# Delta rule and two feed-forward layers on one core: low weight parts among the rows of a small inverse, one chunk's steps half a unit later, one transpose a unit sooner

## The chip, the core and the metric

The kernel runs on one core of a Trainium2 chip. The metric is the device time of one execution in microseconds (us), as a median over runs. A profiled execution also gives a trace: start and length of each instruction on TensorE (PE in the rows), VectorE (DVE), ScalarE (ACT), GpSimd (POOL), and of the DMA issues on SyncE (SP).

## The reference, cut to what matters

```python
for t in range(S):                                  # S = 768, per batch (4) and head (8), D = 48
    y[t]  = q[t] @ state
    v_old = state @ k_n[t]                          # k_n: k over its norm
    state = state + beta[t] * outer(k_n[t], v[t] - v_old)
x = y, heads side by side                           # 3072 tokens x 384
h = x @ w_in;   x1 = (h if h > 0 else exp(h) - 1) @ w_out     # d_ff = 2048
h = x1 @ w2_in; out = (h * sigmoid(1.702 * h)) @ w2_out
```

## The kernel before

**Feed-forward.** The 3072 tokens are six passes p of 512. The work is cut into units, one for each layer, pass and block m of 128 of the 2048 inner features; 16 units make a pass, 192 are all. In a unit `up` makes nine 128x512 products into the tile `h` (L785), ScalarE and VectorE turn `h` into `t` and split it into a high part `gh` (L817, ScalarE) and a low part `gl` (L820, VectorE), and two units later (LAG = 2) `down` makes nine products into `acc` (L832). Each number is carried as high and low part, so a product of two numbers is three matmuls: high-high, low-high, high-low. Weights are split too. For block m VectorE puts bits together (`shift` L750, `rest` L753), ScalarE casts the high part (`high`, L760), VectorE subtracts (`low`, L764). The third matmul of `up` is the first to read the low part. At the end of a pass `end_x1` copies the three sums `acc` out: sum 0 and half of sum 1 on VectorE (L893), sum 2 and then the other half of sum 1 on ScalarE (L891). The next pass's `down` writes the same three banks.

**Delta rule.** Tokens are also cut into 12 chunks c of 64, two to a pass. For each pass a triangular inverse is made on VectorE: `take`, `diag`, `norm`, `scale`, then rows (for passes 0 to 2 a "fine" inverse of 14 row steps, L332 and L337 each; for later ones 30 steps, L322 and L327), then `finish` (L344, L345) and a closing transpose `turn` (L351). The fine ones are then joined by `join16`: `turned` (L399), `left` (L410 on TensorE, L414 on ScalarE), `right` (L425). Chunks follow with `kq` (L519), the diagonal steps `t2`, `m1` (L457, L459), `m2` (L472), then `ks` (L587), `w` (L604), `state` (L627, added up in L635), `ya`, `yb` (L664, L680). `kq`, `m2`, `ks`, `w`, `state` and `ya`/`yb` share one wide place `ps_w` in the accumulation memory. `gram` (L218) reads the keys of a chunk from a tile with tag `kg`.

**What sets the order.** Every engine works through its own list in the order in which the code writes it. The pool `ap` has one buffer for a tag unless told otherwise, and the closing transpose of pass 2 writes a tile with tag `kg`, the same buffer from which the grams of chunks 6 and 7 are read. In unit t the code goes: `up(t)`, ScalarE's first half, the list `fill[t]`, `gl` of unit t-1, the list `mid[t]`, VectorE's first step on `t`, `down(t-2)`, the list `end[t]`, the cast to `gh`, the list `tail[t]`. A slot s of a chunk is half a unit: even slots go to `mid` of unit s/2, odd ones to `end`. In pass 2 (chunks 4 and 5) slots count from unit 16. Gram 6 stands in `end` of unit 16, gram 7 in `end` of unit 17, the first half of `join16` of chunk 4 in `mid` of unit 18. The first two inverses are made ahead of the units, except for the rows of the second, which are the list `beside`.

## Time and profile before

| what | us |
|---|---|
| median of 3 runs (lowest, highest) | 964.88 (964.67, 966.6) |
| profiled execution, its own time | 963.57 |
| its span in the trace | 961.8 |
| TensorE busy in the span | 933.4 (97%) |
| VectorE busy | 589.7 (61%) |
| ScalarE busy | 466.1 (48%) |

The span runs from the first to the last instruction; 1.77 us of the profiled execution's time lie around it. In a row of a timeline stand: start in us, length in us, engine, line, operation, tile written <- tiles read, sizes, count, and in brackets how long the engine had been idle before it and what released it. Where a row has a count over one, its length covers them all.

### The profile page before, as it was taken

How to read it: one execution, taken by the hardware profiler on the slowest of the kernel's cores; microseconds unless marked ns; L12 is line 12 of the kernel's file. 1: busy time of each engine (PE TensorE's matmuls, PEld its weight loads, DVE VectorE, ACT ScalarE, POOL GpSimd, SP SyncE). 2: the span in 40 equal slices, each digit the busy share in tenths (PEclk: the TensorE clock that was granted, in tenths of full speed). 3: DMA queues.
4: the chain of work that ended last, by engine and by line, in shares of the span. 5: the costliest groups of instructions: out<-in, count | busy, mean ns of one | idle time of the engine just before them, and what ended most of it. 6: DMA issues, size and time to landing. Idle time of an engine off the chain costs nothing.

```text
span 961.8 us, 25675 instructions
## 1 busy us (share of the span) xinstructions
PE 933.4 (97%) x11529; PEld 766.2 (80%) x11529; DVE 589.7 (61%) x1061; ACT 466.1 (48%) x751; POOL 59.6 (6%) x62
## 2 busy tenths in 40 slices
PE   5888999999999999999999999999999999999998
PEld 4866777788878878887888888888888888888886
DVE  6989997778788877884346766633333333333333
ACT  6777766444654464444447765433333333333332
POOL 3111200100010010000000101001001001010000
PEclk9999999999999999999999999999999999999999
DMA  7475444022211302111019310010020000100000
GB/s 227 156 220 161 116 139 118 4 79 64 94 57 57 90 36 79 63 49 36 1 68 366 158 66 1 1 66 0 1 66 1 34 33 0 66 1 1 34 1 33
DMA packets 22046, 68.33 MB, mean 71 GB/s; under 512 B 3376, under 2 KB 4912, under 8 KB 21936
## 3 DMA queue, kind: packets, MB, share of 16 engines
q1 hardware_dynamic: 18768, 58.30, 18.2%
q10 hardware_dynamic: 3168, 8.39, 3.0%
q8 instruction: 90, 1.47, 0.6%
q14 instruction: 20, 0.16, 0.1%
HBM read 57.25 MB, written 9.44 MB: 69 GB/s over the span
## 4 chain that ended last, share of the span: by engine, by line
PE 86%; DVE 8%; ACT 2%; issue 2%; DMA 1%; DVEq 0%
PE h L785 38%; PE acc L832 27%; PE accn L832 10%; PE ps_w L587 1%; PE ps_w L604 1%; PE ps_w L519 1%; PE ps_w L664 1%; PE ps_w L680 1%; PE ps_w L627 1%; DVE tmp L332 1%; DVE W L337 1%; DVE gl L820 1%; DVE t L808 1%; ACT z L208 1%; DVE x L540 1%
## 5 line engine op out<-in xcount | busy, mean ns | idle before, releaser
L785 PE MATMUL h<-xh,wt 128*128 128x512 f32 (+1 forms) x1158 | 393.1, 394 | 2.2 <-DVE wt L764 1.8
L832 PE MATMUL acc<-gh,wt 128*128 128x512 f32 x864 | 292.5, 393 | 0.0
L785 PEld LDWEIGHTS h<-xh,wt 128*128 128x128 f32 x1158 | 216.8, 188 | 49.8 <-DVE wt L764 2.9
L785 PE MATMUL h<-xl,wt 128*128 128x512 f32 (+1 forms) x579 | 225.5, 389 | 0.6 <-DVE xl L691 0.6
L820 DVE TENSOR_TENSOR gl<-t,gh 128x512 fp32r<-128x512 f32 x192 | 138.4, 721 | 86.0 <-ACT gh L817 86.0
L832 PEld LDWEIGHTS acc<-gh,wt 128*128 128x128 f32 x864 | 162.3, 188 | 34.6
L817 ACT CAST gh<-t 128x512 fp32r<-128x512 f32 x192 | 119.2, 621 | 126.6 <-DVE t L808 67.8
L832 PE MATMUL acc<-gl,wt 128*128 128x512 f32 x432 | 168.7, 390 | 0.0
L814 DVE TENSOR_TENSOR t<-t,h 128x512 f32<-128x512 f32 x96 | 66.0, 688 | 163.9 <-ACT t L811 163.7
L811 ACT ACTIVATE t<-h 128x512 f32<-128x512 f32 x96 | 57.3, 597 | 184.5 <-PE h L785 184.3
L785 PEld LDWEIGHTS h<-xl,wt 128*128 128x128 f32 x579 | 108.8, 188 | 21.7 <-DVE xl L691 0.8
L804 ACT ACTIVATE t<-h 128x512 f32<-128x512 f32 x96 | 57.3, 597 | 87.7 <-PE h L785 87.2
L832 PE MATMUL accn<-gh,wt 128*128 128x512 f32 x288 | 96.5, 389 | 0.0
L808 DVE SCALAR_TENSOR_TENSOR t<-t,h 128x512 f32<-128x512 f32 x96 | 65.6, 684 | 48.3 <-ACT t L805 47.9
L832 PEld LDWEIGHTS acc<-gl,wt 128*128 128x128 f32 x432 | 81.2, 188 | 16.5 <-DVE gl L820 0.4
L832 PEld LDWEIGHTS accn<-gh,wt 128*128 128x128 f32 x288 | 54.1, 188 | 11.2
L805 ACT ACTIVATE t<-t 128x512 f32<-128x512 f32 x96 | 60.7, 632 | 3.1
L832 PE MATMUL accn<-gl,wt 128*128 128x512 f32 x144 | 56.1, 389 | 0.0
L859 POOL TENSOR_TENSOR xl<-x1r,xh 128x512 fp32r<-128x512 f32 x18 | 23.6, 1309 | 405.3 <-ACT xh L858 314.1
L753 DVE SCALAR_TENSOR_TENSOR w<-raw,w 128x768 uint32<-128x768 uint32 x32 | 32.8, 1026 | 0.8
L760 ACT CAST wt<-w 128x768 fp32r<-128x768 f32 x32 | 26.5, 827 | 12.9 <-DVE w L753 12.8
L327 DVE TENSOR_TENSOR W<-W,tmp 128x30 f32<-128x30 f32 (+14 forms) x90 | 29.9, 333 | 3.1
(206 smaller groups left out, 809.9 us busy)
## 6 DMA issues: line engine op xcount, KB each, us to landing
raw<-in_w SPq DMA_DIRECT2D x19, 768.0 KB, 9.6
raw<-in_w ACTq DMA_DIRECT2D x21, 384.0 KB, 3.1
kt<-in_kT SPq DMA_DIRECT2D x12, 512.0 KB, 4.2
x<-in_qT SPq DMA_DIRECT2D x24, 256.0 KB, 4.3
kn<-in_kn SPq DMA_DIRECT2D x12, 384.0 KB, 3.4
x1d<-xo SPq DMA_DIRECT2D x12, 384.0 KB, 2.6
x1r<-x1d SPq DMA_DIRECT2D x6, 768.0 KB, 5.3
vn<-in_vn SPq DMA_DIRECT2D x11, 384.0 KB, 3.6
```

Source lines behind the costliest of these rows:

```text
L327: v.tensor_tensor(out=w, in0=w, in1=t, op=ALU.add)
L753: v.scalar_tensor_tensor(out=bits[m], in0=words(m, 0), scalar=29, in1=bits[m], op0=ALU.logical_shift_right, op1=ALU.bitwise_or)
L760: nc.scalar.copy(wt[:, 0], bits[m].bitcast(F32))
L785: self.nc.tensor.matmul(hps[:, r], wt[:, part, k * P:(k + 1) * P], src[:, k, r], start=(i == 0), stop=(i == 3 * NK - 1))
L804: nc.scalar.activation(out=t, in_=hps, func=AF.Relu, scale=-1.0)
L805: nc.scalar.activation(out=t, in_=t, func=AF.Exp, scale=-1.0)
L808: nc.vector.scalar_tensor_tensor(out=t, in0=t, scalar=-1.0, in1=hps, op0=ALU.add, op1=ALU.max)
L811: nc.scalar.activation(out=t, in_=hps, func=AF.Sigmoid, scale=1.702)
L814: nc.vector.tensor_tensor(out=t, in0=t, in1=hps, op=ALU.mult)
L817: nc.scalar.copy(gh, t)
L820: nc.vector.tensor_tensor(out=gl, in0=t, in1=gh.bitcast(F32), op=ALU.subtract)
L832: self.nc.tensor.matmul(self.acc[c], wt[:, part, DM + c * P:DM + (c + 1) * P], src, start=(m == 0 and i == 0), stop=(m == NM - 1 and i == 2),)
```

## The change

Three places of the order are changed; no instruction is added or removed, and no DMA moves in its queue.

1. The low parts of weight blocks 4 and 5, which stood at the head of `fill` in units 3 and 4, go to `end` of units 2 and 3, between rows of the second inverse. Those rows go two to `fill` of unit 0 (none were there), five to unit 1, then four around the low part of block 4 in unit 2 (five before), three around that of block 5 in unit 3 (four before). The last two steps (`finish`, `turn`) stay in unit 4.
2. In pass 2 the steps of chunk 4 from `m1` on, and those of chunk 5 up to `state`, go half a unit later, and `m2` a whole one, behind `ks`. `kq` and `ya`/`yb` of chunk 5 stay.
3. `turn` of the third inverse (pass 2) goes from `fill` of unit 18 to the end of `fill` of unit 17.

```diff
+        lows = {}
         for m in range(2, NM):
             shift, rest, low = conv[3 * m - 1:3 * m + 2]
-            at(fill, m - 2, *((low, shift, rest) if m > 2 else (shift, rest, low)))
+            lows[m - 1] = low
+            at(fill, m - 2, *((low,) if m - 1 not in (1, 4, 5) else ()), shift, rest)
+            if m == 2:
+                at(fill, 0, low)
...
-        for u, n in ((1, 5), (2, 5), (3, 4), (4, 2)):
+        for where, u, n in ((fill, 0, 2), (end, 1, 5), (end, 2, 2), (end, 2, 0), (end, 2, 2), (end, 3, 1), (end, 3, 0), (end, 3, 2), (end, 4, 2)):
             for _ in range(n):
-                at(end, u, beside.pop(0)[1])
+                at(where, u, beside.pop(0)[1])
+            if not n:
+                at(end, u, lows[u + 2])
...
-                (8, a, "kq"), (9, a, "t2"), (10, a, "m1"), (12, a, "ks"), (11, a, "m2"), (14, a, "w"),
+                (8, a, "kq"), (9, a, "t2"), (11, a, "m1"), (12, a, "ks"), (13, a, "m2"), (15, a, "w"),
...
-            late = 2 if p in self.FINE else int(p == NP - 1)
+            late = 3 if p in self.FINE else int(p == NP - 1)
...
-        if p == 2:
-            at(fill, steps[1], steps_of.pop())
-            sizes.pop()
-        spread(fill, *steps, steps_of, sizes)
+        turn = [steps_of.pop()] if p == 2 else []
+        spread(fill, *steps, steps_of, sizes[:len(steps_of)])
+        at(fill, steps[1] - 1, *turn)
```

The first place is VectorE in units 2 and 3; the rows with tile `W` are the second inverse's, and `wt` in the row L764 is the low part, of block 4 at its first showing and of block 5 at its second.

```order
+L764 TENSOR_TENSOR wt<-w,wt 128x768
 L332 TENSOR_TENSOR tmp<-W 128x100
 L337 TENSOR_TENSOR W<-W,tmp 128x2x5x10
-L764 TENSOR_TENSOR wt<-w,wt 128x768
-L750 TENSOR_SCALAR w<-raw 128x768
-L753 SCALAR_TENSOR_TENSOR w<-raw,w 128x768
-L820 TENSOR_TENSOR gl<-t,gh 128x512
-L808 SCALAR_TENSOR_TENSOR t<-t,h 128x512
 L332 TENSOR_TENSOR tmp<-W 128x88
 L337 TENSOR_TENSOR W<-W,tmp 128x2x4x11
```

The low part of block 4 stood behind row step 10 (the one of 100 elements) and now stands ahead of it; rows 6 and 7, which used to stand ahead of it in the same unit, are by then done in the unit before.

The second place is VectorE at units 17 and 18, around the third inverse's transpose into `kg`; `acc` numbers are the sums of pass 0, copied out as `xo`.

```order
 L344 MEMSET W 128x32
 L345 TENSOR_TENSOR W<-W,f 128x2x16x16
-L820 TENSOR_TENSOR gl<-t,gh 128x512
-L808 SCALAR_TENSOR_TENSOR t<-t,h 128x512
-L893 COPY xo<-acc_1254 128x512
-L893 COPY xo<-acc_1255 128x256
 L351 STREAM_TRANSPOSE kg<-W 128x32x32
+L820 TENSOR_TENSOR gl<-t,gh 128x512
+L808 SCALAR_TENSOR_TENSOR t<-t,h 128x512
+L893 COPY xo<-acc_1258 128x512
+L893 COPY xo<-acc_1259 128x256
```

The transpose moved ahead of four instructions: the low part `gl` of unit 16, the step on `t` of unit 17 and both copies of the sums. ScalarE's and TensorE's lists are the same there before and after.

The third place is ScalarE behind chunk 4's `m1`; `L475` copies the result of `m2` out of `ps_w`.

```order
 L460 COPY m_3265<-ps_b 128x512
 L461 COPY z<-z 128x32x32
+L817 CAST gh<-t 128x512
+L804 ACTIVATE t<-h 128x512
+L805 ACTIVATE t<-t 128x512
 L475 ACTIVATE z<-ps_w 32x2x16x32 x2
-L817 CAST gh<-t 128x512
-L804 ACTIVATE t<-h 128x512
-L805 ACTIVATE t<-t 128x512
```

The copy of `m2` moved one unit behind: a cast and the two activations of a unit now stand between `m1`'s copies and it.

## Rows read from the trace of the kernel before

**Rows 1.** The page's first section: busy us, share of the span, instructions.

```profile
PE 933.4 (97%) x11529; PEld 766.2 (80%) x11529; DVE 589.7 (61%) x1061; ACT 466.1 (48%) x751; POOL 59.6 (6%) x62
```

**Rows 2.** Timeline of VectorE, units 0 to 4.

```profile
61.65 0.69 DVE L808 SCALAR_TENSOR_TENSOR t<-t,h 128x512 f32<-128x512 f32 x1 [0.82 <-ACT t L805]
...
65.91 0.19 DVE L332 TENSOR_TENSOR tmp<-W 128x28 f32<-128x28 f32 x1
...
66.88 0.23 DVE L332 TENSOR_TENSOR tmp<-W 128x72 f32<-128x72 f32 x1
...
68.81 0.96 DVE L764 TENSOR_TENSOR wt<-w,wt 128x768 fp32r<-128x768 f32 x1 [0.26 <-ACT wt L760]
...
72.35 0.26 DVE L332 TENSOR_TENSOR tmp<-W 128x108 f32<-128x108 f32 x1
...
73.57 0.28 DVE L332 TENSOR_TENSOR tmp<-W 128x112 f32<-128x112 f32 x1
...
75.28 0.95 DVE L764 TENSOR_TENSOR wt<-w,wt 128x768 fp32r<-128x768 f32 x1
...
84.45 1.05 DVE L345 TENSOR_TENSOR W<-W,f 128x512 f32<-128x512 f32 x1
85.53 2.05 DVE L351 STREAM_TRANSPOSE xl<-W 128x1024 f32<-128x1024 f32 x1
```

**Rows 3.** Timeline of TensorE, ScalarE and GpSimd, units 3 to 5.

```profile
76.29 0.73 PE L785 MATMUL h<-xh,wt 128*128 128x512 f32 x2 [1.83 <-DVE wt L764]
...
78.93 0.62 ACT L817 CAST gh<-t 128x512 fp32r<-128x512 f32 x1 [0.37 <-DVE t L808]
...
81.40 2.34 ACT L530 COPY x<-ps_w 64x512 f32<-64x512 f32 x4
...
83.80 0.94 PE L627 MATMUL ps_w<-su,kn 64*48 64x48 f32 x64 [0.17 <-ACT x L530]
...
83.82 2.68 POOL L533 TENSOR_SCALAR_AFFINE_SELECT x<-x 64x1024 f32<-64x1024 f32 x2 [28.81 <-ACT x L530]
...
87.63 1.26 PE L410 MATMUL ps_b<-xl,z 32*32 32x16 f32 x128 [0.63 <-DVE xl L351]
```

**Rows 4.** Timeline of all engines at the third inverse's transpose, units 17 and 18.

```profile
159.09 0.69 DVE L345 TENSOR_TENSOR W<-W,f 128x512 f32<-128x512 f32 x1
...
161.64 1.16 PE L218 MATMUL ps_w<-kg 48*64 48x64 f32 x64 [0.34 <-DMA kg<-in_kT]
...
162.76 1.02 DVE L893 COPY xo<-acc 128x512 f32<-128x512 f32 x2
163.69 2.02 DVE L351 STREAM_TRANSPOSE kg<-W 128x1024 f32<-128x1024 f32 x1
...
163.81 0.37 ACT L891 COPY xo<-acc 128x256 f32<-128x256 f32 x1 [1.21 <-DVE xo L893]
164.08 1.02 ACT L205 COPY z<-ps_w 128x1024 f32<-128x1024 f32 x1
...
165.76 1.26 PE L410 MATMUL ps_b<-kg,z 32*32 32x16 f32 x128 [0.69 <-DVE kg L351]
...
168.97 0.35 ACT L414 COPY m<-ps_b 128x256 f32<-128x256 f32 x1
...
169.38 0.61 PEld L425 LDWEIGHTS ps_b<-m,t 16*32 16x32 f32 x63 [0.51 <-ACT m L414]
```

**Rows 5.** Timeline of TensorE and VectorE around chunk 4's `m2` and chunk 5's `state`.

```profile
190.11 0.22 PE L472 MATMUL ps_w<-m,kg 32*32 32x32 f32 x2 [0.29 <-issue]
...
193.62 0.69 DVE L820 TENSOR_TENSOR gl<-t,gh 128x512 fp32r<-128x512 f32 x1 [0.33 <-ACT gh L817]
194.22 0.95 DVE L592 TENSOR_TENSOR vn<-vn,ps_w 128x768 f32<-128x768 f32 x1
...
196.27 0.39 PE L785 MATMUL h<-xh,wt 128*128 128x512 f32 x1
...
224.92 2.25 DVE L635 TENSOR_TENSOR su<-su,ps_w 48x384 f32<-48x384 f32 x4 [0.92 <-PE ps_w L627]
```

## Prediction

> **What bounds the kernel now.** I read the page's first section first: TensorE is busy for 933.4 of 961.8 us [rows 1]. So the time moves only where a wait of TensorE goes or a new one comes. I then read TensorE's timeline at the three places that the change touches, for the brackets, and the timelines of VectorE and ScalarE beside it, for what ended each. At unit 4, `up` stands 1.83 us for the low part of block 4; then 0.17 at `state` of chunk 1 for ScalarE's copies of a mask, and 0.63 at `left` of chunk 2 for the second inverse's transpose [rows 3]. At the third inverse's transpose `left` of chunk 4 stands 0.69 [rows 4], and `m2` of chunk 4 stops for 0.29 for no reason that the rows give [rows 5]. These five make 3.61 us, which is all that the change could take from TensorE's waits here. The terms below are made against the profiled execution (963.57, a span of 961.8 and 1.77 around it); the median of the runs, 964.88, is 1.31 above it, and I carry the sum over to the median.

> **Part 1, the low parts among the rows.** Two row steps go ahead of VectorE's step on `t` of unit 0, where it idled 0.82 [rows 2]. Two of them take 66.88 - 65.91 = 0.97, so what follows is about 0.1 late (0.15 at most). In unit 1 the five rows are now steps 3 to 7 and not 1 to 5: steps 6 and 7 take 73.57 - 72.35 = 1.22 against 0.97 for 1 and 2, and the 0.25 more fit into the 0.26 for which the next low part waited. In unit 2 the low part of block 4 began 75.28 - 72.35 = 2.93 behind the first row. Two rows of about 1.22 now stand ahead of it and not five: 1.7 sooner, less the 0.1: 1.6. TensorE's stand of 1.83 would shrink to 0.2.

> What is late next? `state` of chunk 1 (83.80) needs the place that ScalarE's four copies (81.40 to 83.74) read [rows 3]. Ahead of them ScalarE stood idle once, 0.37 at the cast of unit 3, for VectorE's step on `t`. That step comes sooner too, so at best the 0.37 go, and I take 0.35: `state` at 83.45. From `state` to `left` TensorE has 87.63 - 0.63 - 83.80 = 3.20 of its own work, so `left` could begin at 86.65. It also needs the second inverse's transpose. VectorE is ahead there by rows 6 and 7 (1.22), less the 0.1 and a short new wait for ScalarE at the step of unit 3, which I put at 0.1: 1.0. The transpose ends at 85.53 + 2.05 - 1.0 = 86.58. Both ways give `left` at about 86.65, so TensorE gains 0.98 for good. The ends are 0.35 (the transpose comes no sooner than `state` does) and 1.6 (nothing takes from the first gain).

> The work on VectorE has a neighbour. Scaling the inverse (L345) took 1.05 beside GpSimd's selection, which began at 83.82 [rows 2, 3]; the same form alone took 0.69 [rows 4]. In the new order L345 would begin at 83.4 and the selection, released by the copies, at 83.47. If the selection is first by those 0.07, L345 loses between the 0.36 of the row and one selection, 2.68 / 2 = 1.34, and the term falls to between 0.6 and 0. [...] This is a rival below.

> **Part 3, the transpose one unit sooner.** It writes the buffer from which gram 7 reads its keys, so it must wait for the last product of that gram; the program gives it that wait, on the same count of TensorE, before and after. Before, the wait was long over: gram 7 ran 161.64 to 162.80, itself released by its keys' DMA, and the transpose's turn came at 163.69 [rows 4]. Now it stands behind L345, which ends at 159.09 + 0.69 = 159.78. VectorE would stand there for some 3 us, until about 162.87, and transpose until 164.89 (2.02). Queued behind it are the low part `gl` of unit 16, the step on `t` of unit 17 and both copies of sums. From `gl` to the next instruction is 194.22 - 193.62 = 0.60 [rows 5], and the step on `t` takes as long: copies from 166.0 to 167.02, where they ended at 163.78. That is 3.24 later.

> Who waits for them? ScalarE's half of sum 1 (L891) began 0.03 after the copies, having waited 1.21; it goes to 167.05. Behind it ScalarE's list runs without a bracket to L414, which copies what `left` made: L205 at 164.08, its other copies, a cast, two activations, L414 at 168.97 to 169.32. All of it goes 3.24 later, L414 to 172.21. `right` (L425) on TensorE waited for L414 before, if briefly (its weights row shows 0.51) and began at 169.38; it now begins at 172.62. The 0.69 that `left` no longer waits buys nothing, since `right` hangs on ScalarE and not on `left`. `down` of unit 16 waits for the copies of the sums too, but is done by then. So part 3 costs 3.24. Behind it no bracket of TensorE in the pass is over 0.3, so nothing gives the time back.

> That ScalarE and VectorE do not pass a waiting instruction shows in a row: L205's input was complete at 162.80, ScalarE was idle for 1.21 us before 163.81, and L205 still began only behind L891, at 164.08 [rows 4]. [...]

> **Part 2, half a unit later.** Between the end of `up` of unit 21 and the beginning of `up` of unit 23 (196.27, [rows 5]) TensorE has the same seven batches, now with `m2` last. `m2` is 128 small products; as many took 1.26 at L410 [rows 4]. So if nothing waits it begins between 194.5 and 195.0. It now needs the place that `ks` used, which L592 frees; that ended at 194.22 + 0.95 = 195.17, after 0.33 of waiting for a cast that stood behind the copy of `m2` and no longer does [rows 5]: 194.84. So `m2` waits 0 to 0.3, and its old stop of 0.29 may stay or go. Further on `kq` of chunk 5 now follows `state` with nine products between them. The sums of L635 take 2.25, the nine products 3.20 - 0.94 = 2.26 [rows 3, 5]: a wait of 0 to 0.2. The other steps keep a unit or more between maker and reader, and the moved DMAs (the next `vn` and `kn`, released by `w` and `state`) come half a unit later with readers that are as much later. The term is between -0.3 and +0.5; I take +0.2.

> **Sum.** -0.98 + 3.24 + 0.2 = +2.46: the profiled execution's 963.57 becomes 966.0, the median's 964.88 becomes 967.3.

> **The rivals.**

> *VectorE is not held (not slower).* The transpose runs from 159.6 or so, when VectorE idles anyway, and ends before the copies' old turn. For it: its data are ready then. Against it: gram 7 reads the same buffer until 162.80. Each microsecond that the transpose begins after 159.63 (163.78 less the 4.15, from 162.87 to 167.02, that it, `gl`, the step and the copies take) costs one. Part 3 then costs 0.1 and not -0.69, because `right` hangs on L414: -0.98 + 0.1 + 0.2 = -0.7, 964.2. The point from which it decides is a beginning at 160.4, where the gain of part 1 is used up.

> *GpSimd's selection comes first.* The first term falls to about 0.3: +3.1, 968.0. For it speaks the row of 1.05; against it that the two beginnings lie within 0.07 and may fall either way.

> *All gains are kept and VectorE is not held.* Then part 1 brings its 1.6 and `m2` loses its stop: -1.6 + 0.1 - 0.3 = -1.8, 963.1. Against it: `state` hangs on ScalarE, which gains 0.37 at most.

> **How the numbers follow.** The forecast has 0.58, with a range of its own of 966.4 to 968.3; the transpose not held 0.14; the selection first 0.14; all gains kept 0.08; 0.06 is left for what I don't see. 963.8 to 968.8 takes in the first three with the bounds of their terms (the last case and half of the unseen lie outside). About 0.2% (1.93 us) is what a measurement of this kernel can tell from no change: slower begins at 966.8. Of the forecast some 0.5 lie above that, and nearly all of the selection case: 0.63 slower. Faster by as much, below 962.95, needs all gains and a little more: 0.09. The rest, 0.28, is within.

> **What would show it.** Right: at unit 4 the bracket of 1.83 down to about 0.2, `left` of chunk 2 about 1.0 us sooner; the transpose L351 directly behind L345 with a bracket of about 3 us that names TensorE's gram (L218); L891 with a bracket of over 4 us; L425 with one of over 3 us for ScalarE's L414. Wrong: if L351 begins within 0.3 of L345's end, part 3 is free and the forecast falls; if L425 waits long but the span doesn't grow by it, TensorE got the time back behind it; if L345 at unit 4 takes over 1.2, the selection was first.

## The result, and the profile after

The changed kernel takes 973.17 us (median; 969.04 to 979.62), the kernel before beside it 964.58. The ratio is 1.0085, with a 95% interval of [1.0065, 1.0105]: slower by 6.3 to 10.1 us, where 2.5 were forecast, and above the range. A second set of runs gave 973.0, ratio 1.009 [1.006, 1.0119].

The profiled execution is the slowest of its set (979.62, span 977.9). First the line of its page with the busy times, then its windows: the stretch, its length, the busy us of the five engines (with counts), the granted clock of TensorE (PEclk), and share and rate of the DMA. In what follows a *stand* is a stretch in which TensorE waits for another engine, a *stop* one that the profile puts to no engine (`issue`).

```profile
PE 943.7 (97%) x11529; PEld 774.4 (79%) x11529; DVE 588.6 (60%) x1061; ACT 466.5 (48%) x751; POOL 59.7 (6%) x62
```

```profile
85.00:91.00 6.00, 4.30 (x80) 3.23 (x79) 5.79 (x13) 5.93 (x11) 1.46 (x1) 1.00 0.67 190
91.00:95.00 4.00, 4.00 (x110) 2.87 (x110) 3.97 (x5) 2.11 (x4) 1.29 (x2) 0.57 0.83 274
...
104.00:109.00 5.00, 5.00 (x74) 3.77 (x74) 4.59 (x7) 1.83 (x4) 0.00 (x0) 0.66 0.35 91
109.00:179.00 70.00, 67.35 (x1487) 53.65 (x1485) 55.64 (x109) 44.91 (x66) 6.06 (x6) 1.00 0.41 121
179.00:187.00 8.00, 5.80 (x138) 4.95 (x139) 4.48 (x7) 3.02 (x6) 0.00 (x0) 0.57 0.01 2
187.00:220.00 33.00, 30.82 (x839) 24.42 (x841) 19.85 (x40) 15.26 (x24) 3.15 (x3) 1.00 0.05 15
```

TensorE is busy 10.3 us longer than in [rows 1] for the same 11529 products. Part of that is clock: near 91, 104 and 180 it falls to its lower level, which is half (0.50 in the windows of the first experiment); a window shows a mean, so 0.57 of 8 us means some 6.9 us at half. In the trace of before it is 1.00 throughout these units, but that was one of the better executions: of 64 others of the kernel before, run beside the experiments, 11 have a mean granted clock of 1.000 and the rest less. Now the timeline at the places of [rows 2 to 5]:

```profile
64.47 0.38 PE L785 MATMUL h<-xh,wt 128*128 128x256 f32 x1
...
87.13 2.34 ACT L530 COPY x<-ps_w 64x512 f32<-64x512 f32 x4
...
89.46 0.69 DVE L345 TENSOR_TENSOR W<-W,f 128x512 f32<-128x512 f32 x1
89.52 0.94 PE L627 MATMUL ps_w<-su,kn 64*48 64x48 f32 x64 [1.70 <-ACT x L530]
90.19 2.08 DVE L351 STREAM_TRANSPOSE xl<-W 128x1024 f32<-128x1024 f32 x1
...
93.92 1.48 PE L410 MATMUL ps_b<-xl,z 32*32 32x16 f32 x128
...
167.44 0.69 DVE L345 TENSOR_TENSOR W<-W,f 128x512 f32<-128x512 f32 x1
170.20 1.16 PE L218 MATMUL ps_w<-kg 48*64 48x64 f32 x64 [0.54 <-DMA kg<-in_kT]
171.47 2.08 DVE L351 STREAM_TRANSPOSE kg<-W 128x1024 f32<-128x1024 f32 x1 [3.34 <-PE ps_w L218]
173.61 1.26 PE L410 MATMUL ps_b<-kg,z 32*32 32x16 f32 x128
174.59 1.02 DVE L893 COPY xo<-acc 128x512 f32<-128x512 f32 x2
175.42 0.47 PE L832 MATMUL acc<-gh,wt 128*128 128x512 f32 x1 [0.55 <-DVE xo L893]
175.64 0.37 ACT L891 COPY xo<-acc 128x256 f32<-128x256 f32 x1 [4.69 <-DVE xo L893]
180.79 0.35 ACT L414 COPY m<-ps_b 128x256 f32<-128x256 f32 x1
181.20 1.90 PE L425 MATMUL ps_b<-m,t 16*32 16x16 f32 x128 [3.46 <-ACT m L414]
...
211.54 0.22 PE L472 MATMUL ps_w<-z,m 32*32 32x32 f32 x2 [2.18 <-issue]
...
245.00 1.16 PE L519 MATMUL ps_w<-x,kt 48*64 48x64 f32 x64 [0.15 <-issue]
```

The forecast's chain is there link by link: the transpose stands 3.34 behind gram 7, the copies come late, ScalarE's L891 has a bracket of 4.69, and `right` (L425) stands 3.46 for L414. From gram 7 (170.20) to `right` (181.20) are 11.00; in [rows 4] it was 169.38 - 161.64 = 7.74, so 3.26 more, where the forecast has 3.24. Two things are not in the forecast: by the end of that stand the clock has halved (L425 takes 1.90 where 128 small products took 1.26 at L410 in [rows 4]), and inside `m2` TensorE stops 2.18 for its next instruction. Row 64.47 is 6.4 us later than the same product of before; nothing ahead of it was changed.

### The profile page after: what moved, and what is told of

Its sections match the earlier page's. It is cut to its first block, busy times and chain, and to the rows that moved or that the text cites. A ratio compares the mean times of both kernels' runs of the same rounds, so it can differ in the third digit from the quotient of the medians.

```text
span 977.9 us, 25677 instructions
## 1 busy us (share of the span) xinstructions
PE 943.7 (97%) x11529; PEld 774.4 (79%) x11529; DVE 588.6 (60%) x1061; ACT 466.5 (48%) x751; POOL 59.7 (6%) x62
## 4 chain that ended last, share of the span: by engine, by line
PE 90%; DVE 3%; ACT 3%; DMA 2%; issue 1%; SPq 0%; ACTq 0%; DVEq 0%
PE h L785 39%; PE acc L832 29%; PE accn L832 10%; PE ps_w L587 1%; PE ps_w L604 1%; PE ps_w L519 1%; DMA kt<-in_kT 1%; PE ps_w L664 1%; PE ps_w L680 1%; PE ps_w L627 1%; PE ps_w L218 1%; PE ps_w L472 1%; PE ps_b L425 1%; ACT z L208 1%; DMA kg<-in_kT 0%
## 5 line engine op out<-in xcount | busy, mean ns | idle before, releaser
L820 DVE TENSOR_TENSOR gl<-t,gh 128x512 fp32r<-128x512 f32 x192 | 138.3, 720 | 93.0 <-ACT gh L817 92.9
L753 DVE SCALAR_TENSOR_TENSOR w<-raw,w 128x768 uint32<-128x768 uint32 x32 | 32.8, 1026 | 0.8
```

Of the source, the lines that this page charges most:

```text
L753: v.scalar_tensor_tensor(out=bits[m], in0=words(m, 0), scalar=29, in1=bits[m], op0=ALU.logical_shift_right, op1=ALU.bitwise_or)
L820: nc.vector.tensor_tensor(out=gl, in0=t, in1=gh.bitcast(F32), op=ALU.subtract)
```

## The experiments

Twelve runs were made in three sets; medians of the kernel before in them were 965.0, 965.34 and 964.87, and ratios are to those runs. Of each edit the lines that matter are shown.

**Part 3 alone.** 971.04 us, ratio 1.0059 [1.0044, 1.0074].

```diff
...
+        turn = [steps_of.pop()] if p == 2 else []
+        spread(fill, *steps, steps_of, sizes[:len(steps_of)])
+        at(fill, steps[1] - 1, *turn)
```

> The kernel before with part 3 alone (third inverse's transpose a unit sooner). Theory A (the transpose is held by chunk 7's gram; ScalarE and TensorE's right of chunk 4 come 3.24 us later; after that stand TensorE's clock is granted at half for some us): L425 of chunk 4 with a bracket of 3.2 to 3.6 us, a stretch of granted clock under 1 right behind it, +4.5 to +6 us in all. Theory B (the 3.24 alone, the clock's fall belongs to something else): +3.0 to +3.6 us and a clock of 1.0 between 160 and 200 us. Theory C (the loss of the changed kernel lies in the first 60 us and in the clock there, not in the transpose): within 1 us of the kernel before.

Its timeline and windows:

```profile
162.87 1.16 PE L218 MATMUL ps_w<-kg 48*64 48x64 f32 x64 [0.76 <-DMA kg<-in_kT]
168.09 0.47 PE L832 MATMUL acc<-gh,wt 128*128 128x512 f32 x1 [0.55 <-DVE xo L893]
173.88 1.91 PE L425 MATMUL ps_b<-m,t 16*32 16x16 f32 x128 [3.47 <-ACT m L414]
```

```profile
172.00:173.00 1.00, 0.00 (x0) 0.00 (x0) 0.69 (x2) 0.94 (x3) 0.00 (x0) 0.83 0.00 0
173.00:174.00 1.00, 0.12 (x8) 0.12 (x12) 1.00 (x3) 1.00 (x3) 0.00 (x0) 0.50 0.00 0
174.00:178.00 4.00, 4.00 (x133) 3.49 (x133) 2.43 (x5) 0.74 (x2) 0.00 (x0) 0.50 0.02 4
178.00:179.00 1.00, 1.00 (x4) 0.79 (x3) 0.36 (x1) 0.00 (x0) 0.00 (x0) 0.50 0.00 0
179.00:180.00 1.00, 1.00 (x5) 0.82 (x4) 0.00 (x0) 0.19 (x1) 0.00 (x0) 0.76 0.00 0
```

From gram 7 to `right` are 173.88 - 162.87 = 11.01, 3.27 more than the 7.74 of [rows 4]: the forecast's term. TensorE then works from 173.88 to about 179.5 at half clock, which loses half of 5.6: 2.8 at most. Together 6.1, and the medians differ by 6.04.

**Part 1 alone.** 965.1, ratio 1.0 [0.9987, 1.0013].

```diff
...
+            at(fill, m - 2, *((low,) if m - 1 not in (1, 4, 5) else ()), shift, rest)
...
+            if not n:
+                at(end, u, lows[u + 2])
```

> The kernel before with part 1 alone (low parts of blocks 4 and 5 among the rows). Theory A: up of unit 4 loses its wait of 1.83, state of chunk 1 waits 1.4 to 1.7 for ScalarE's mask copies, left of chunk 2 no longer waits, the clock stays at 1.0: -0.8 to -1.1 us. Theory B (the wait at state, now longer in one piece, makes the clock fall between 85 and 110 us as in the changed kernel): the clock falls there and the time is +0.5 to +3 us. Theory C: what is lost before unit 0 comes with this part: the first product of unit 0 later than 61 us.

```profile
83.62 0.94 PE L627 MATMUL ps_w<-su,kn 64*48 64x48 f32 x64 [1.70 <-ACT x L530]
86.75 1.11 PE L410 MATMUL ps_b<-xl,z 32*32 32x16 f32 x111
88.80 0.32 PE L410 MATMUL ps_b<-xl,z 32*32 32x16 f32 x17 [0.94 <-issue]
```

`state` and `left` begin at 83.62 and 86.75, forecast 83.45 and 86.65. Then `left` stops for an instruction for 0.94, which before it did not: nearly all of the 0.88 won at 86.75 is gone. The stop is in five of the six profiles that have part 1 as it stands (0.47 to 0.94) and in none of the seven without it. The interval (-1.3 to +1.3 us) would still hold the -0.98 of the forecast; that the gain did not last is read from the profiles.

**Part 2 alone.** 968.38, ratio 1.0026 [1.0006, 1.0046].

```diff
-                (8, a, "kq"), (9, a, "t2"), (10, a, "m1"), (12, a, "ks"), (11, a, "m2"), (14, a, "w"),
+                (8, a, "kq"), (9, a, "t2"), (11, a, "m1"), (12, a, "ks"), (13, a, "m2"), (15, a, "w"),
...
-            late = 2 if p in self.FINE else int(p == NP - 1)
+            late = 3 if p in self.FINE else int(p == NP - 1)
```

> The kernel before with part 2 alone (chunk 4 and 5 half a unit later). Theory A: only the stop inside m2 of chunk 4 changes (0.29 us before, 2.2 in the changed kernel), +1.5 to +2.2 us. Theory B: that stop came from the stand at the transpose ahead of it; alone the part costs 0 to 0.5 us and m2's stop is under 0.5.

```profile
203.04 0.21 PE L472 MATMUL ps_w<-z,m 32*32 32x32 f32 x2 [2.27 <-issue]
```

`ks` of chunk 4 keeps its slot (12), though the list of the change reads as if it moved with the others; so `m2` passes it. The stop inside `m2` is here too: it belongs to part 2. The ten executions run from 964.42 to 972.21. This profile (971.23) is 7.7 behind that of before at its last product, and 4.6 of that arises ahead of 63.7 us, where nothing was changed. Part 2 lies between 183 and 234 us, where TensorE loses 2.2. Another 1.2 goes at 158 to 183 us, where the clock is lower for 3.4 us although the long stand of part 3 isn't there:

```profile
170.00:180.00 10.00, 10.00 (x273) 7.91 (x260) 4.95 (x8) 5.40 (x10) 0.00 (x0) 0.83 0.07 27
```

**Parts 1 and 2.** 967.28, ratio 1.0015 [0.9999, 1.0032].

```diff
...
+            at(fill, m - 2, *((low,) if m - 1 not in (1, 4, 5) else ()), shift, rest)
...
+            late = 3 if p in self.FINE else int(p == NP - 1)
```

> Parts 1 and 2 without part 3 (the transpose stays where it was). Theory A: the changed kernel less the hold and less the clock's fall behind it: 4.5 to 6 us faster than the changed kernel, no bracket over 0.5 at L425 of chunk 4, clock 1.0 from 160 to 200 us. Theory C (loss in the first 110 us): still 3 us or more slower than the kernel before.

2.3 above the kernel before by the medians. This profile has no stop in `m2`, so the stop does not come in every execution. Its clock was expected at 1.00 from 160 to 200 us; it is at the lower level for 3.4 us from 169.9, without the long stand.

**The changed kernel again.** 973.0, ratio 1.009 [1.006, 1.0119]; nothing is edited.

> The changed kernel once more, nothing edited, for a second profile and more times. Theory A (the loss comes from the stand behind the held transpose, from the clock behind that stand and from the stop inside m2; the 5.7 us by which the first profile was late ahead of unit 0 are chance): the median is about 973 again, the first product of the second half of up(0) begins near 58 us in most executions, and the profile shows the stand of about 3.4 us at L425 with a half-clock stretch behind it. Theory B (the early lateness belongs to the changed kernel): it begins near 64 us again.

```profile
57.04 0.38 PE L785 MATMUL h<-xh,wt 128*128 128x256 f32 x1
...
171.44 1.91 PE L425 MATMUL ps_b<-m,t 16*32 16x16 f32 x128 [3.46 <-ACT m L414]
...
202.20 0.21 PE L472 MATMUL ps_w<-z,m 32*32 32x32 f32 x2 [2.47 <-issue]
```

This execution took 970.4. Its row at 57.04 stood at 64.47 in the first profile: the early lateness is scatter between executions. The stand, the slow L425 and the stop are in both.

**Part 3 without the hold.** 967.04, ratio 1.0017 [1.0001, 1.0034]. The transpose writes a buffer of tag `kt`; for that the keys `kt` of chunks 4 and 5 are loaded three and five units later (not shown).

```diff
...
-            t = spare[1][:, 0:1024] if p < 2 else self.ap.tile([P, 1024], F32, name="kg", tag="kg")
+            t = spare[1][:, 0:1024] if p < 2 else self.ap.tile([P, 1024], F32, name="kt", tag="kt", bufs=2)
```

> Part 3 alone, with the closing transpose of pass 2 in a buffer of tag kt in place of kg, so that no gram holds it (the keys kt of chunks 4 and 5 are loaded 3 and 5 units later for it). Theory A (the hold is all of part 3's cost): L351 begins within 0.3 us of the end of L345, the stand of 3.47 us at L425 and the half clock behind it go, and the time is 963.5 to 965.5, that of the kernel before or a little less. Theory B (the place costs, by what it pushes back on VectorE): 967 or more.

```profile
160.21 0.69 DVE L345 TENSOR_TENSOR W<-W,f 128x512 f32<-128x512 f32 x1
161.00 2.09 DVE L351 STREAM_TRANSPOSE kt<-W 128x1024 f32<-128x1024 f32 x1
...
164.11 1.03 DVE L893 COPY xo<-acc 128x512 f32<-128x512 f32 x2
...
170.75 0.71 PE L425 MATMUL ps_b<-m,t 16*32 16x16 f32 x62 [1.51 <-ACT m L414]
```

L351 begins 0.10 behind the end of L345, so the hold is gone as the first theory has it, but the time is that of the second: part 3 costs 1.7 [0.1, 3.3] in place of 6.0, where I had expected nothing. TensorE no longer waits at `left`; it waits 1.51 at L425 instead. In this profile the clock is 0.83 in the ten microseconds from 170, which is 3.4 at half, 1.7 lost. The run with both cures, below, has the same wait of 1.51 without the lower clock, and there TensorE leaves this place no later than before: by these two profiles what remains of part 3 is the clock and not the place.

**Stands by themselves.** 1000.22, ratio 1.0364 [1.034, 1.0389]. In layer 2, where the kernel before runs units of 18 products of 128x512 without a wait, n dummy multiplications on VectorE (and a memset) delay the low part.

```diff
...
+                nc.vector.tensor_tensor(out=j, in0=j, in1=j, op=ALU.mult)
...
+        for u, n in ((125, 12), (141, 13), (157, 14), (173, 15), (189, 17)):
+            at(fill, u, lambda n=n: busy(n))
```

> The kernel before, with dummy products on VectorE (12, 13, 14, 15 and 17 of 128x512, and a memset) ahead of the low part in units 125, 141, 157, 173 and 189 of layer 2, where the kernel before has neither waits nor small matmuls. Worked out from rows of the kernel before (0.60 us for each, 6.1 us of slack), TensorE should stand about 1.1, 1.7, 2.3, 2.9 and 4.1 us, 12 us in all. Theory A (behind a long stand the granted clock falls and costs again): half-clock stretches directly behind the longer stands and none elsewhere in layer 2, and the time grows by the stands plus half of those stretches, some 16 to 21 us in all. Theory B (a stand costs its length): plus 12 us, the clock full throughout.

```profile
693.68 0.50 PE L832 MATMUL acc<-gl,wt 128*128 128x512 f32 x1 [2.95 <-DVE gl L820]
...
836.16 0.79 PE L832 MATMUL acc<-gl,wt 128*128 128x512 f32 x1 [4.40 <-DVE gl L820]
```

```profile
675.00:694.00 19.00, 16.05 (x71) 12.99 (x70) 13.46 (x20) 4.05 (x7) 1.29 (x1) 1.00 0.00 1
694.00:698.00 4.00, 4.00 (x12) 3.15 (x11) 2.20 (x4) 1.73 (x3) 0.00 (x0) 0.57 0.00 0
698.00:760.00 62.00, 62.00 (x275) 51.33 (x274) 26.41 (x38) 20.07 (x34) 3.88 (x3) 1.00 0.08 26
```

The stands were longer than worked out, 2.95 to 6.58, and so is the time: 34.9 us, above both theories. With each of the five there is a stretch of lower clock (3.4 us with those of 2.95, 3.67 and 5.13, 6.8 with those of 4.40 and 6.58, by the windows), which begins behind the stand or late in it, and while TensorE works on layer 2 there is none elsewhere.

**Shorter stands.** 974.25, ratio 1.0093 [1.0059, 1.0127]. The edit is against the run above.

```diff
-        for u, n in ((125, 12), (141, 13), (157, 14), (173, 15), (189, 17)):
+        for u, n in ((125, 9), (141, 9), (157, 10), (173, 10), (189, 11)):
```

> The run with dummy products in layer 2 again, with 9, 9, 10, 10 and 11 of them. By the rows of that run (2.95 us of stand for 12, and 0.73 more for each one more) TensorE should stand about 0.77, 0.77, 1.5, 1.5 and 2.2 us, 6.7 us in all. Theory A (a shorter stand is followed by a lower clock less often): half-clock stretches behind some of the five or none, the time up by 6.7 to 12. Theory B (each stand of any length draws one): five stretches, up by 15 or more.

```profile
889.57 0.50 PE L832 MATMUL accn<-gl,wt 128*128 128x512 f32 x1 [1.49 <-DVE gl L820]
...
957.36 0.74 PE L832 MATMUL acc<-gl,wt 128*128 128x512 f32 x1 [2.22 <-DVE gl L820]
```

```profile
884.00:892.00 8.00, 6.51 (x29) 5.05 (x29) 7.11 (x11) 1.58 (x3) 0.00 (x0) 1.00 0.00 0
...
957.30:961.00 3.70, 3.64 (x9) 2.90 (x10) 2.33 (x5) 1.74 (x3) 0.00 (x0) 0.54 0.00 0
```

Only the last of the five draws the lower clock. What each stand of both kernels cost is how much later a product 60 behind it begins, against the same one of the kernel before, than one 40 ahead of it (behind the last stand of each run only 43 products are left, and the last of them is taken):

| stand, us | 0.77 (twice) | 1.49 (twice) | 2.22 | 2.95 | 3.67 | 4.40 | 5.13 | 6.58 |
|---|---|---|---|---|---|---|---|---|
| cost, us | 1.07 | 1.79 | 4.11 | 4.86 | 5.61 | 7.00 | 7.01 | 9.21 |

The four short ones cost 0.30 beyond their length, the others 1.9 to 2.6. VectorE has its dummy work in all ten, so that work alone does not lower the clock. The sums, 33.7 and 9.8, lie in the intervals of the two ratios (32.8 to 37.6, 5.7 to 12.3).

**Part 2 with `m2` ahead of `ks`.** 966.27, ratio 1.0012 [0.9996, 1.0027]. The edit is against part 2 alone.

```diff
-                (8, a, "kq"), (9, a, "t2"), (11, a, "m1"), (12, a, "ks"), (13, a, "m2"), (15, a, "w"),
+                (8, a, "kq"), (9, a, "t2"), (11, a, "m1"), (13, a, "ks"), (12, a, "m2"), (15, a, "w"),
```

> Part 2 alone, but with m2 of chunk 4 left ahead of ks, as in the kernel before (m1 in slot 11, m2 in 12, ks in 13). Theory A (part 2 costs through the stop inside m2 at its new place behind ks, 2.27 us in the profile of part 2 alone): no such stop, 965 to 966.5. Theory B (the rest of the shift costs, or the early lateness does): 968 and as wide a scatter as part 2 alone.

`m2` runs without a stop. By the medians (0.9 above before in place of 3.4) 2.5 are gone, but the intervals of the two ratios overlap, so this pair of times doesn't settle it. The profiles say more: between 183 and 234 us TensorE lost 2.20 with part 2 alone and gains 0.26 here.

**The changed kernel with `m2` ahead of `ks`.** 969.44, ratio 1.0054 [1.0033, 1.0076]: the same line in the changed kernel.

> The changed kernel with m2 of chunk 4 put back ahead of ks (m1 in slot 11, m2 in 12, ks in 13; all else as changed). Theory A (the stop inside m2, 2.18 and 2.47 us in two profiles, belongs to m2's place behind ks): no stop inside m2 and 970 to 971.5, some 2 us below the changed kernel's 973. Theory B (the stop is chance, or another batch takes it over): 973 still, with a stop of over 1.5 us in a neighbouring batch of small products.

4.6 above the kernel before by the medians, where the changed kernel in its second set is 7.7 above: 3.1 less, and the stop that is gone from `m2` was 2.18 and 2.47. Again the intervals overlap, but both pairs point the same way, and between 183 and 234 us this profile loses 0.09 where the two of the changed kernel lose 2.13 and 2.50. The second theory's stop in a neighbouring batch is not there.

**Both cures.** The changed kernel with `m2` ahead of `ks` and the transpose in a buffer of tag `kt`: 966.61, ratio 1.0011 [0.9994, 1.0029].

```diff
...
+                (8, a, "kq"), (9, a, "t2"), (11, a, "m1"), (13, a, "ks"), (12, a, "m2"), (15, a, "w"),
...
+            t = spare[1][:, 0:1024] if p < 2 else self.ap.tile([P, 1024], F32, name="kt", tag="kt", bufs=2)
```

> The changed kernel with m2 put back ahead of ks and the closing transpose of pass 2 in the buffer of tag kt (keys of chunks 4 and 5 loaded later for it). If the costs are the hold with the clock behind it (971.04 against 967.04 for part 3 alone: 4.0) and the stop in m2 (2.2), the time is 973 - 6.2 = 966.8, between 965.5 and 968. If a third cost of 2 us or more is hidden in the combination: 969 or more.

```profile
169.60 1.26 PE L425 MATMUL ps_b<-m,t 16*32 16x16 f32 x128 [1.51 <-ACT m L414]
```

966.8 was worked out, 966.61 came, so there is no sign of a third cost of 2 us. This execution took 963.68; it has the stand of 1.51 of the run without the hold, but its clock is 1.00 behind it and L425 takes 1.26.

**Part 1 with `state` half a unit later.** 968.5, ratio 1.0035 [1.0021, 1.0049]. The edit is against part 1 alone.

```diff
-            (10, 1, "state"), (8, 2, "kq"), (8, 2, "mask"), (13, 2, "nv"), (14, 3, "kq"), (14, 3, "mask"), (15, 2, "t2"),
+            (11, 1, "state"), (8, 2, "kq"), (8, 2, "mask"), (13, 2, "nv"), (14, 3, "kq"), (14, 3, "mask"), (15, 2, "t2"),
```

> Part 1 alone, with state of chunk 1 half a unit later (slot 11 in place of 10), behind the nine products of down and half of left, so that ScalarE's copies of the mask are over when it comes. Theory A (part 1 gained nothing because state stood 1.70 us for those copies in place of up for the low part): that bracket goes and the time is 963.5 to 964.3, about 1 us below part 1 alone (965.1). Theory B (something behind it, the transpose of the second inverse at left, takes the time back): 965 again, with a bracket of about 1 us at left of chunk 2.

```profile
86.19 1.33 PE L410 MATMUL ps_b<-xl,z 32*32 32x16 f32 x128 [1.34 <-DVE xl L351]
...
91.24 0.58 PE L627 MATMUL ps_w<-su,kn 64*48 64x48 f32 x17 [2.59 <-issue]
```

```profile
87.00:101.00 14.00, 11.41 (x263) 9.08 (x252) 9.82 (x16) 6.49 (x11) 0.00 (x0) 0.51 0.50 141
```

A miss for both theories: the bracket for ScalarE is gone, but `left` now stands 1.34 for the transpose (as the second theory had it), and `state`, directly behind a batch of small products, stops 2.59 for its next instruction. The clock falls behind the first of the two and stays at its lower level for 13.7 us, half of which is 6.8. Between 63.7 and 158 us this profile loses 5.5, and none of the ten executions has a mean clock above 0.996.

## Why the prediction was wrong, step by step

| term | forecast | measured alone, by the medians [by the interval] |
|---|---|---|
| part 1 | -0.98 | +0.1 [-1.3, +1.3] |
| part 2 | +0.2 | +3.4 [+0.6, +4.4] |
| part 3 | +3.24 | +6.0 [+4.2, +7.1] |
| sum | +2.46 | +8.6 [+6.3, +10.1] in the first set |

The profiles say where the time goes. The change alters the order of TensorE's products only within 185 to 227 us, so the same product, counted from the start, can be sought in two traces. The table has how much TensorE loses against the trace of before (minus: gains) in each stretch of that trace, and in brackets for how many us the clock was at its lower level there (columns behind 63.7):

| profile | to 63.7 | 63.7 to 157.7 | 157.7 to 183.1 | 183.1 to 233.7 | to the end |
|---|---|---|---|---|---|
| changed kernel, first | 5.71 | 2.65 (6.8) | 5.44 (6.8) | 2.13 | 0.13 |
| changed kernel, second | -0.81 | 0.01 | 4.88 (6.8) | 2.50 | 0.25 |
| the same, `m2` ahead of `ks` | 0.51 | -0.37 | 6.63 (6.8) | 0.09 | 1.09 |
| part 3 alone | 1.65 | -0.84 | 6.16 (6.8) | -0.08 | 0.46 |
| part 3 without the hold | -0.03 | 1.15 (3.4) | 2.42 (3.4) | -0.05 | 0.38 |
| part 2 alone | 4.61 | -0.61 | 1.20 (3.4) | 2.20 | 0.27 |
| parts 1 and 2 | 0.16 | 2.44 (3.4) | 1.40 (3.4) | -0.29 | 0.11 |
| part 1 alone | 0.11 | -0.29 | -0.27 | 0.05 | 0.40 |
| both cures | 0.16 | -0.19 | -0.13 | -0.27 | 0.53 |

**Part 3: the mechanism was right, the size was off.** The hold, the late copies, L891, L414 and L425 came as worked out, and `right` was 3.27 later behind gram 7. The step that failed is "So part 3 costs 3.24. Behind it no bracket of TensorE in the pass is over 0.3, so nothing gives the time back." It looked for time given back and not for time taken again, and its premise, "So the time moves only where a wait of TensorE goes or a new one comes", has no place for the clock. By the end of the stand the clock is at its lower level, in all four profiles that have this stand (6.8 us of it in 170 to 180 or 180 to 190, windows of 0.66 in three and 0.70 in the fourth), and in this stretch these four lose 4.88 to 6.63. A stand of 3.67 in a dense stream costs 5.61, so 6.0 fits the stand and the clock that goes with it. VectorE and ScalarE kept to their order here: in the first profile L820's cast ended at 169.19 and L820 began at 173.39, behind the transpose, and L205, whose gram ended at 171.36, began at 175.90, behind L891. In layer 2 each of the six stands of 2.22 to 6.58 went with 3.4 or 6.8 us of lower clock, and the four of 0.77 and 1.49 with none. Near 170 us, among batches of small products, short waits are followed by 3.4 us of lower clock in some executions and not in others: one of 1.07 at `left` in part 2 alone (1.20 lost) but not in the run with `state` half a unit later, one of 1.51 at L425 without the hold (2.42 lost) but not with both cures.

**Part 2: one stop was mis-sized.** The step is "its old stop of 0.29 may stay or go": in its new place `m2` stops for 2.18, 2.27 and 2.47 in three of the four profiles that have it behind `ks`, and for less than 0.1 in the three shifted ones that have it ahead. The stretch from 183 to 234 us loses 2.13 to 2.50 in those three and between -0.29 and 0.09 in the four others, so the stop is the whole of it. The rest of the +3.4 of the medians is not shown to be part 2's: that profile had lost 5.2 ahead of it. The two waits that the term was made of were small, as forecast: 0.15 at `kq`, none ahead of `m2`. What is left of part 2 with `m2` ahead of `ks`, +0.9 [-0.4, +2.6], can't be told from no change.

**Part 1: right as far as it went.** The bracket of 1.83 at `up` went (to nothing, 0.2 was forecast), `state` hung on ScalarE's copies, `left` came 0.88 sooner. The step that failed is "so TensorE gains 0.98 for good": a stop of 0.94 inside `left` took it back. In the four profiles with part 1 and a full clock, the stretch from 63.7 to 157.7 us gains 0.37 at most. In the first profile stretches of lower clock from 91 and 105 hid even that.

**The rivals.** VectorE was held (it stood 3.34); with the transpose in a buffer that no gram holds part 3 cost 1.7 [0.1, 3.3], where the rival has 0.1, an estimate that no run shows. L345 at unit 4 took 0.69 and began at 89.46, the selection at 89.54, so GpSimd's selection did not come first; behind a selection that began first (83.82, [rows 3]) it took 1.05, and no run shows the loss of 1.34 that the low end of the term needs. Every rival was about a wait for another engine; most of what was missing is the clock and the supply of instructions, which none of them has.

**Open.** Why the instructions for `m2` come late there and not one batch earlier, and why one profile of four has no stop, no run shows; the last section has how late they came. What decides whether a wait of 1 to 2 us is followed by a lower clock stays open too. The early lateness of the first profile (5.7 at 63.7 us) and of part 2 alone (4.6) was not traced to a cause; the second profile of the changed kernel lacks it.

## What to carry to other kernels

A new stand of two or three microseconds on TensorE is to be priced with what the clock does behind it: here a stand that made `right` 3.27 later cost 6.0, and in a dense stream one of 2.95 cost 4.86. When two short waits (0.69 and 0.51 in [rows 4]) merge into one, the time can grow by more than the brackets: with one of 1.51 in their place 2.42 were lost in the profile without the hold, which has 3.4 us of lower clock there, and none with both cures, where the clock is 1.00. So read the granted clock of the window at each long bracket, in more than one execution. And a step that moves a batch of small products next to another one can stop TensorE for want of instructions, here for 2.18 to 2.47 in three profiles of four, without any bracket that names an engine.

## What the runs showed of the hardware

The stops marked "issue" inside batches of small products lie on a grid. Counting TensorE's products, those of 0.29 us or more behind the first 50 us have 1238, 1366, 1874, 2002, 2130, 3787, 4299, 4427, 4554 or 5828 products ahead of them in the various profiles: always a whole number of steps of 127 or 128 apart (1874 to 2002 are 128, 4427 to 4554 are 127), whatever batch stands there. The page of after has a queue of its own for instructions:

```profile
q8 instruction: 90, 1.47, 0.6%
```
